# Three rational-function groups with b folded into two activation scales, and a new order of all steps

## The chip, the cores and the metric

One core of a Trainium2 chip runs the whole program. Its engines work side by side, each through its own list of instructions in order: TensorE (PE, matmuls into PSUM), VectorE (DVE), ScalarE (ACT), GpSimd (POOL, here mostly to start DMAs) and SyncE (SP, loads and stores). Semaphores tie them together. The metric is the device time of one execution in microseconds (us). Before the change the median of three runs is 264.83 us (264.46 to 264.94).

## The reference

```python
# attention with a polynomial feature map; q, k, v: (4 batches, 4 heads, 1088, 32), S1, S2: (8, 32)
def phi(x):
    a = einsum('rd,bhsd->bhsr', S1, x); b = einsum('rd,bhsd->bhsr', S2, x)
    return einsum('bhsi,bhsj->bhsij', a, b).reshape(..., 64)
kv  = einsum('bhsf,bhsd->bhfd', phi(k), v);  z = sum(phi(k), axis=2)
x   = einsum('bhsf,bhfd->bhsd', phi(q), kv) / (einsum('bhsf,bhf->bhs', phi(q), z) + 1e-6)
# then, over 4352 tokens of 128 features, w_in: (128, 2048), w_out: (2048, 128), a: (4,), b: (2,)
h = x @ w_in
P = a[0] + a[1]*h + a[2]*h**2 + a[3]*h**3
Q = 1 + |b[0]|*|h| + |b[1]|*h**2
out = (P / (Q + 1e-6)) @ w_out
```

## The kernel before, in words

The 4352 tokens are cut into ten chunks: two of 256 tokens, seven of 512, and one of 256 with the 64 leftover tokens of each batch. For each batch the key side (steps `k tr`, `k ev`, `k ab`, `k eva`, `k prod`, `kv`, `kv rem`, `kvbd`, `zbd`, `zproj`, `zspread`, `zrem`) builds kv and z; for each chunk the query side (`q tr`, `q ev`, `q abc`, `q eva`, for batches after the first a division `q dpr`, `q dsum`, `q dinv`, `q scale`, then `q prod`, `qp tr`, `qp ev`, `x mm`, `x ev`) gives the transposed x. The first two chunks, called 0 and 0b, go a slightly different way (`nd`, `div add`, `div inv`, `div`, `x tr`).

The second half works on groups: one chunk and up to eight blocks of 128 of the 2048 hidden features, so that a full group is a tile of 128 x 4096. There are 23 groups (0 to 22); 4 to 18 are full. A group g runs

- `h g,s` (PE, line 794): h = x @ w_in, two blocks at a time, into one of two PSUM tiles `h_ps`;
- `hev g,s` (ACT, line 800): h_ps to bf16 `hb`;
- the even part of Q into `u`, `ln g` and `exp g` (ACT, lines 833 and 837): u = exp(-ln(u + 1 + 1e-6)) = 1/Q;
- P into `y` (DVE), `n5 g` (DVE, line 829): y = y * u, and `py g` (PE, line 857): y @ w_out, summed in `out_ps`; then `oev`, `otr`, `otev` and a store.

The table `TERMS` gives each group one of four forms. Two matter here. Form "t" (groups 5, 7, 11, 13, 16, 18) takes |h| on DVE. Form "s" (groups 4, 9, 14) takes it on ACT. Before the change a group of form "s" has these steps:

- `habs` (ACT, line 809): u = |h * |b0||;
- `sq` (DVE, line 914): lin A = h * h;
- `sqb` (DVE, line 919): lin B = A * |b1|;
- `dq` (a DMA that POOL starts, line 897): u += B, after `habs` and `sqb`;
- `n1` (DVE, line 925): y = a3 * A + a1, and `n3` (DVE, line 925): A = a2 * A + a0, in place;
- `n2` (DVE): y = y * hb; `dy` (a DMA from POOL): y += A; then `ln`, `exp`, `n5`, `py`.

In form "t" the logarithm has a scale of its own, `b_rel[:, 0:1]`, a value per partition; in form "s" its scale is the constant 1. `lin` has two buffers, `hb`, `u` and `y` three each, `L` (between `ln` and `exp`) one.

Nothing is scheduled at run time. `plan.add` collects the steps in a fixed numbering, and `plan.issue` runs through the list `ORDER` and emits step after step, so `ORDER` alone decides in which order each engine meets its work. `HOT` is a list of blocks of dummy matmuls on a spare PSUM bank (`hot`, line 1075), which keep TensorE busy. b arrives by a load behind that of a (line 245); `abs_b` (line 387) and `rel_b` (lines 391 to 393) make |b0|, |b1| and the quotients from it.

Of the kernel before, what the change touches and what calls it, by code (L numbers as in the profile page):

```python
# [12 lines left out]
FP = mybir.dt.float32  # L13
BF = mybir.dt.bfloat16
# [5 lines left out]
    0, 2, 53, 4, 5, 1, 3, 54, 6, 8, 10, 55, 7, 9, 11, 12, 14, 13, 16, 15, 17, 70, 75, 56, 71, 18, 76, 72, 77, 52,  # L20
    19, 20, 73, 80, 22, 57, 24, 21, 23, 26, 25, 68, 78, 28, 69, 30, 74, 81, 97, 82, 27, 79, 85, 29, 98, 83, 84, 31,
    99, 86, 87, 88, 100, 101, 91, 102, 104, 89, 90, 103, 105, 106, 92, 113, 107, 108, 114, 109, 115, 110, 116, 111,
    117, 129, 112, 297, 60, 32, 130, 298, 118, 67, 119, 120, 65, 64, 311, 122, 121, 62, 34, 312, 123, 63, 299, 36,
    144, 325, 93, 124, 33, 125, 126, 319, 313, 61, 145, 66, 58, 127, 296, 300, 320, 146, 128, 301, 326, 94, 147,
    305, 302, 359, 321, 314, 95, 35, 306, 37, 96, 361, 38, 322, 315, 303, 316, 333, 40, 360, 200, 327, 334, 131,
    362, 317, 59, 148, 328, 363, 132, 307, 308, 365, 150, 304, 201, 39, 364, 133, 134, 309, 310, 162, 366, 318, 42,
    151, 135, 339, 136, 163, 323, 335, 137, 41, 43, 367, 329, 138, 324, 368, 369, 152, 153, 149, 166, 374, 336, 341,
    340, 167, 139, 342, 202, 154, 376, 140, 343, 155, 349, 141, 44, 142, 350, 375, 203, 351, 156, 330, 188, 157,
    158, 331, 143, 45, 189, 385, 337, 370, 377, 371, 190, 386, 159, 332, 352, 191, 387, 160, 204, 46, 161, 192, 164,
    344, 168, 378, 389, 372, 165, 388, 169, 391, 345, 211, 170, 171, 172, 390, 392, 407, 173, 174, 394, 338, 175,  # L30
    212, 48, 373, 393, 193, 177, 176, 408, 409, 346, 395, 178, 400, 379, 194, 411, 181, 410, 412, 179, 413, 195,
    182, 180, 432, 402, 50, 347, 401, 47, 414, 196, 348, 433, 353, 415, 354, 197, 215, 396, 49, 183, 403, 434, 198,
    397, 184, 398, 435, 404, 421, 416, 436, 438, 216, 437, 51, 439, 422, 417, 199, 423, 205, 441, 206, 399, 454,
    456, 440, 355, 185, 455, 442, 207, 237, 380, 238, 457, 405, 208, 424, 243, 209, 447, 458, 418, 210, 356, 460,
    448, 244, 381, 449, 213, 357, 425, 459, 214, 461, 217, 186, 218, 406, 443, 219, 462, 468, 450, 187, 479, 419,
    444, 480, 245, 445, 220, 481, 469, 382, 482, 483, 221, 463, 420, 246, 484, 426, 451, 222, 239, 247, 446, 501,
    485, 240, 486, 502, 464, 470, 427, 223, 452, 224, 505, 488, 489, 487, 490, 503, 225, 471, 504, 226, 494, 227,
    491, 230, 228, 507, 495, 428, 506, 229, 241, 526, 496, 465, 508, 358, 527, 453, 472, 528, 515, 530, 509, 466,
    467, 529, 383, 516, 510, 497, 473, 531, 532, 498, 548, 492, 231, 474, 533, 242, 232, 429, 517, 493, 233, 550,
    234, 549, 475, 511, 535, 551, 534, 536, 518, 512, 537, 541, 499, 235, 552, 553, 554, 236, 500, 543, 542, 248,  # L40
    538, 555, 519, 573, 513, 562, 575, 574, 476, 430, 556, 281, 576, 384, 577, 539, 544, 578, 563, 557, 545, 579,
    520, 558, 514, 564, 580, 282, 521, 565, 477, 582, 255, 249, 581, 583, 595, 540, 256, 250, 259, 251, 252, 596,
    588, 584, 253, 597, 254, 559, 257, 260, 601, 258, 589, 261, 590, 585, 546, 283, 598, 262, 263, 264, 522, 265,
# [80 lines left out]
def kernel(  # L124
# [13 lines left out]
    nc = tc.nc  # L138
# [23 lines left out]
    HOT = [2, 6, 23, 4, 18, 4, 3]  # L162
# [152 lines left out]
    b_rel = consts.tile([128, 3], FP, name="b_rel")  # L315
# [74 lines left out]
    def rel_b():  # L390
        nc.vector.tensor_scalar(out=b_rel[:, 0:1], in0=b_abs[:, 0:1], scalar1=1e-18, scalar2=None, op0=AX.max)
        nc.vector.reciprocal(out=b_rel[:, 1:2], in_=b_rel[:, 0:1])
        nc.vector.tensor_mul(out=b_rel[:, 2:3], in0=b_rel[:, 1:2], in1=b_abs[:, 1:2])

    c_b = plan.add("DVE", 100, abs_b, after=[ld["ab"]], rank=-5)
    c_b = plan.add("DVE", 300, rel_b, after=[c_b], rank=-5) if "t" in USED else c_b
# [187 lines left out]
    def add_queries(n, nt, srcs, weights, kv_lhs, load_steps, kv_steps, w_steps, rank, give=(), early=False,  # L584
# [58 lines left out]
        def product():  # L643
            abc = T["abc", n][:, :G, :]
            T["q_p", n] = tile_of(att, "q_p", [128, JC * H, R * R], FP)
            nc.vector.tensor_mul(out=T["q_p", n][:, :G, :].rearrange("p g (i j) -> p g i j", i=R),
                                 in0=abc[:, :, 0:R, None].broadcast_to([128, G, R, R]),
                                 in1=abc[:, :, None, R:2 * R].broadcast_to([128, G, R, R]))
# [69 lines left out]
        def rest(s):  # L718
            s = plan.add("DVE", 68 + 1067 * G // 16, product, after=[s, T.get(("prod", n - 1)) if pair == 1 else None], rank=rank + 0.02, take=["q_p"],
# [59 lines left out]
    def add_group(g, G):  # L779
# [27 lines left out]
        def s_abs():  # L807
            T["u", g] = tile_of(moe, "u", [128, GW], BF)
            nc.scalar.activation(out=T["u", g][:, :gw], in_=T["hb", g][:, :gw], func=ACT.Abs, scale=b_abs[:, 0:1])  # L809
# [21 lines left out]
        def ln(l0, lw):  # L831
            T["L", g, l0] = tile_of(moe, "L", [128, LW], FP)
            nc.scalar.activation(out=T["L", g, l0][:, :lw], in_=T["u", g][:, l0:l0 + lw], func=ACT.Ln, bias=one_ap,  # L833
                                 scale=b_rel[:, 0:1] if terms == "t" else 1.0)
# [278 lines left out]
```

## Time and profile before

| what | value |
|---|---|
| median of three runs | 264.83 us (264.46 to 264.94) |
| the profiled execution's own time | 264.85 us |
| its span, first to last instruction | 263.1 us, so 1.75 us lie around it |
| granted TensorE clock, mean | 0.996 |
| busy: PE, DVE, ACT, POOL | 246.8, 242.8, 238.6, 43.0 us |
| line 919, form "s" (`sqb`) | 3 instructions, 3.9 us |
| the software DMA queue | 25.69 MB, 62.6% of 16 DMA engines' span |

How to read it. A busy share is the time in which an engine executed something, so waiting is not in it; three engines are above 90% at once. "Idle before" tells how long an engine stood still ahead of an instruction and who released it. A mean duration overlaps a little with the next instruction on the same engine, so the distance from start to start is what an instruction really costs its engine. The windows view adds up busy time for stretches of the span; since it can count no more than the stretch, what is missing from a stretch is idle time.

### The profile page before, as it was taken

The numbers are of one execution on the slowest core, as the hardware profiler recorded it, in microseconds if no ns is written. First come the engines' busy times: TensorE is split into PE (matmuls) and PEld (weight loads), VectorE is DVE, ScalarE is ACT, GpSimd is POOL, SyncE is SP. The second block draws the span as 40 slices with busy tenths as digits, with TensorE's granted clock in tenths as the row PEclk, the third lists the DMA queues.
The fourth block names the chain that finished last, engine by engine and source line by source line (L and its number), as shares of the span: only waits on it lengthen the run. The fifth ranks groups of instructions, "written<-read, shape, count | busy, mean of one in ns | idle before, by whom it ended". The sixth has DMA issues, their size and how long they took to land. (4 is left out here: it accounts for less than half of the span.)

```text
span 263.1 us, 3159 instructions
## 1 busy us (share of the span) xinstructions
PE 246.8 (94%) x1186; PEld 145.6 (55%) x1186; DVE 242.8 (92%) x240; ACT 238.6 (91%) x211; POOL 43.0 (16%) x63
## 2 busy tenths in 40 slices
PE   8999999999999999989899998999999899999971
PEld 4889898755656654434373645545434345554451
DVE  1658999979999999999999999999999999999992
ACT  3249798889989999999999999999999999999993
POOL 3700010101201113011201121101220202122000
PEclk9999999999999999999999999999999999999998
DMA  6969839952888996938798879972799896788812
GB/s 171 298 209 174 166 90 173 218 91 50 189 159 96 165 190 93 118 55 150 144 133 139 156 102 181 184 139 50 133 167 128 159 187 84 91 159 162 120 40 101
DMA packets 36607, 36.94 MB, mean 140 GB/s; under 512 B 18160, under 2 KB 30448, under 8 KB 36464
## 3 DMA queue, kind: packets, MB, share of 16 engines
q0 software_dynamic: 11664, 25.69, 62.6%
q1 hardware_dynamic: 24496, 10.95, 15.8%
q8 instruction: 9, 0.15, 0.2%
q10 hardware_dynamic: 432, 0.10, 0.2%
q14 instruction: 6, 0.05, 0.1%
HBM read 8.82 MB, written 2.23 MB: 42 GB/s over the span
## 5 line engine op out<-in xcount | busy, mean ns | idle before, releaser
L794 PE MATMUL h_ps<-xT,w_in_sb 128*128 128x512 f32 (+1 forms) x320 | 126.6, 533 | 0.9 <-ACT hb L800 0.9
L794 PEld LDWEIGHTS h_ps<-xT,w_in_sb 128*128 128x128 f32 x320 | 57.4, 190 | 43.4 <-issue 34.3
L800 ACT CAST hb<-h_ps 128x1024 bf16<-128x1024 f32 (+1 forms) x70 | 70.9, 1038 | 5.6 <-PE h_ps L794 5.4
L837 ACT ACTIVATE u<-L 128x4096 bf16<-128x4096 f32 (+3 forms) x23 | 63.7, 2768 | 0.3
L829 DVE TENSOR_TENSOR y<-y,hb 128x4096 bf16<-128x4096 bf16 (+3 forms) x37 | 58.7, 1595 | 0.1
L833 ACT ACTIVATE L<-u,one_ap 128x4096 f32<-128x4096 bf16 (+3 forms) x17 | 43.4, 2555 | 0.2 <-DVE u L829 0.2
L829 DVE TENSOR_TENSOR y<-y,u 128x4096 bf16<-128x4096 bf16 (+3 forms) x23 | 39.8, 1731 | 0.5 <-ACT u L837 0.3
L857 PEld LDWEIGHTS <-w_out 128*128 128x128 bf16 x208 | 20.2, 98 | 27.6 <-issue 11.8
L857 PE MATMUL out_ps<-y,w_out 128*128 128x512 bf16 (+1 forms) x144 | 30.8, 355 | 1.1 <-DVE y L829 1.1
L897 POOL DMA_DIRECT2D u<-lin x9 | 10.8, 1206 | 104.4 <-ACT ab L461 25.7
L833 ACT ACTIVATE L<-u,one_ap,b_rel 128x4096 f32<-128x4096 bf16 x6 | 23.2, 3875 | 0.0
L914 DVE TENSOR_TENSOR lin<-hb 128x4096 bf16<-128x4096 bf16 x9 | 20.6, 2287 | 0.0
L897 POOL DMA_DIRECT2D y<-lin x9 | 12.0, 1334 | 49.6 <-DVE y L829 15.7
L829 DVE TENSOR_TENSOR u<-lin,u 128x4096 bf16<-128x4096 bf16 (+3 forms) x14 | 19.2, 1375 | 0.2
L897 POOL DMA_DIRECT2D y<-zeros x7 | 12.3, 1760 | 41.6 <-PE h_ps L794 18.4
L820 DVE TENSOR_SCALAR u<-hb 128x4096 int16<-128x4096 int16 (+3 forms) x20 | 18.4, 918 | 0.5 <-ACT hb L800 0.3
L489 PEld LDWEIGHTS kv_ps<-v_aug,k_p 128*128 128x128 f32 x128 | 15.3, 192 | 1.1 <-issue 0.2
L489 PE MATMUL kv_ps<-v_aug,k_p 128*128 128x66 f32 x128 | 15.8, 272 | 0.0
L857 PE MATMUL out_ps<-u,w_out 128*128 128x512 bf16 (+1 forms) x64 | 13.7, 352 | 1.3 <-ACT u L837 1.1
L1075 PE MATMUL kv_ps<-const-float32-0.0 128*128 128x512 bf16 x60 | 14.2, 381 | 0.0
L661 ACT COPY q_pT<-w_ps 128x512 f32<-128x512 f32 (+1 forms) x20 | 10.5, 552 | 2.6 <-PE w_ps L654 2.6
L841 DVE TENSOR_SCALAR y<-hb,a_sb 128x4096 bf16<-128x4096 bf16 (+3 forms) x14 | 12.4, 886 | 0.0
(102 smaller groups left out, 274.1 us busy)
## 6 DMA issues: line engine op xcount, KB each, us to landing
u<-lin POOLq DMA_DIRECT2D x9, 1024.0 KB, 7.9
y<-lin POOLq DMA_DIRECT2D x9, 1024.0 KB, 8.2
y<-zeros POOLq DMA_DIRECT2D x6, 1024.0 KB, 11.0
out_dram<-oT SPq DMA_DIRECT2D x7, 256.0 KB, 2.7
kq<-in_k_dram SPq DMA_DIRECT2D x3, 512.0 KB, 5.0
v_aug<-in_v_dram SPq DMA_DIRECT2D x12, 128.0 KB, 4.7
kq<-in_q_dram SPq DMA_DIRECT2D x3, 512.0 KB, 4.8
w_in_sb<-in_moe_w_in_dram SPq DMA_DIRECT2D x1, 1024.0 KB, 6.9
```

Source lines behind the costliest of these rows:

```text
L489: nc.tensor.matmul(T["kv", b][:, hp * 66:(hp + 1) * 66], lhsT=lhs(hp), rhs=rhs(hp), start=(first and hp == 0), stop=final, skip_group_chec ...
L794: nc.tensor.matmul(T["h", g, s][:, i * W:(i + 1) * W], lhsT=w_in_sb[:, fi * 128:(fi + 1) * 128], rhs=T["xT", n][:, :W], start=True, stop=True)
L800: nc.scalar.copy(out=T["hb", g][:, s * W:(s + nsub) * W], in_=T["h", g, s][:, :nsub * W])
L820: nc.vector.tensor_scalar(out=u().bitcast(mybir.dt.int16), in0=hb().bitcast(mybir.dt.int16), scalar1=0x7FFF, scalar2=None, op0=AX.bitwise_and)
L829: return lambda: nc.vector.tensor_mul(out=out(), in0=in0(), in1=in1())
L833: nc.scalar.activation(out=T["L", g, l0][:, :lw], in_=T["u", g][:, l0:l0 + lw], func=ACT.Ln, bias=one_ap, scale=b_rel[:, 0:1] if terms == ...
L837: nc.scalar.activation(out=T["u", g][:, l0:l0 + lw], in_=T["L", g, l0][:, :lw], func=ACT.Exp, scale=-1.0)
L841: nc.vector.tensor_scalar(out=y(), in0=hb(), scalar1=a_sb[:, 3:4], scalar2=a_sb[:, 2:3], op0=AX.mult, op1=AX.add)
L857: nc.tensor.matmul(T["o", n][:, :W], lhsT=W_terms[w][:, fis[i], :], rhs=T[src, g][:, i * W:(i + 1) * W], start=(start and i == 0), stop=(s ...
L897: nc.gpsimd.dma_start(out=dst(), in_=src(), accum_op=AX.add, max_dma_last_dim=4096)
L914: nc.vector.tensor_mul(out=sq(), in0=hb(), in1=hb())
L1075: nc.tensor.matmul(hot_ps[0], lhsT=zero.broadcast_to([128, 128]), rhs=zero.broadcast_to([128, CW]), start=True, stop=True)
```

## The change

In a group of form "s" Q is divided by |b1| inside: `habs` takes |h| times |b0|/|b1| (`b_rel[:, 5:6]`), the DMA `dq` adds the square itself, and `ln` multiplies by |b1| (`b_rel[:, 1:2]`, a value per partition). `sqb` is gone from the three groups. The square must now outlive `n3`, so `n3` writes its result into the second `lin` buffer, `dq` waits for `n3`, and `dy` adds that second buffer. `rel_b` makes six values with four instructions in place of three values with three. A choice `QPOOL` is added and left empty. `HOT` has 11 blocks with 71 dummy matmuls in place of 7 with 60. `ORDER` is a new list; here are the moves that matter, by engine:

- DVE: `abs_b` and `rel_b` go ahead of `q prod 0b` (before: `abs_b` right behind it, `rel_b` much later); the first steps of groups 0 and 1 are mixed anew; `k prod (3, 0)` goes ahead of `sq 9`; `n5` of groups 4, 7, 16, 18 and some `abs`, `n1` change places with neighbours.
- ACT: `ln 0`, `exp 0` ahead of `hev 2,0`; `k ev ('rem', 1)`, `q ev 2` later; `qp ev 3,1`, `q ev 4`, `oev 0` ahead of `hev 7,4`; `exp 12` ahead of `q eva 8`; `hev 10,0` behind `habs 9`; `hev 19,4` ahead of `ln 17`, so that `exp 17` follows `ln 17` directly.
- PE: `h 3,2` ahead of `h 3,0`; `kv 3,0`, `kv 3,1`, `kv rem 3` of the last batch much earlier, among the blocks of groups 10 and 11 (before: groups 12 to 14), so that `h 10,4` to `h 12,0` stand further back; `hot 0` already among the blocks of group 14 (before: group 17).
- POOL: the copy for `zproj` behind two copies of v. SP: two stores change places; the loads are as before.

```diff
 ORDER = [
...
-    HOT = [2, 6, 23, 4, 18, 4, 3]
+    QPOOL = set()
+    HOT = [5, 4, 1, 6, 3, 19, 13, 6, 7, 4, 3]
...
-    b_rel = consts.tile([128, 3], FP, name="b_rel")
+    b_rel = consts.tile([128, 6], FP, name="b_rel")
...
     def rel_b():
-        nc.vector.tensor_scalar(out=b_rel[:, 0:1], in0=b_abs[:, 0:1], scalar1=1e-18, scalar2=None, op0=AX.max)
-        nc.vector.reciprocal(out=b_rel[:, 1:2], in_=b_rel[:, 0:1])
-        nc.vector.tensor_mul(out=b_rel[:, 2:3], in0=b_rel[:, 1:2], in1=b_abs[:, 1:2])
+        nc.vector.tensor_scalar(out=b_rel[:, 0:2], in0=b_abs[:, 0:2], scalar1=1e-18, scalar2=None, op0=AX.max)
+        nc.vector.reciprocal(out=b_rel[:, 2:4], in_=b_rel[:, 0:2])
+        nc.vector.tensor_mul(out=b_rel[:, 4:5], in0=b_rel[:, 2:3], in1=b_abs[:, 1:2])
+        nc.vector.tensor_mul(out=b_rel[:, 5:6], in0=b_rel[:, 3:4], in1=b_abs[:, 0:1])
...
         def s_abs():
             T["u", g] = tile_of(moe, "u", [128, GW], BF)
-            nc.scalar.activation(out=T["u", g][:, :gw], in_=T["hb", g][:, :gw], func=ACT.Abs, scale=b_abs[:, 0:1])
+            nc.scalar.activation(out=T["u", g][:, :gw], in_=T["hb", g][:, :gw], func=ACT.Abs, scale=b_rel[:, 5:6])
...
             nc.scalar.activation(out=T["L", g, l0][:, :lw], in_=T["u", g][:, l0:l0 + lw], func=ACT.Ln, bias=one_ap,
-                                 scale=b_rel[:, 0:1] if terms == "t" else 1.0)
+                                 scale={"t": b_rel[:, 0:1], "s": b_rel[:, 1:2]}.get(terms, 1.0))
...
         if square:
             sp = plan.add("DVE", tt, s_first, after=[he], rank=g - 0.5, take=["lin"], name=f"sq {g}")
-            d2 = plan.add("DVE", ts + 61, s_scaled, after=[sp, c_b], rank=g - 0.5, take=["lin"], name=f"sqb {g}")
-            d = add_tile("dq", u, even, [ha, d2], g - 0.5, give=["lin"])
+            if wide_abs:
+                d1 = plan.add("DVE", ts + 121, s_affine(y, 3, 1), after=[sp, ld["ab"]], rank=g - 0.45, take=["y"], name=f"n1 {g}")
+                t = plan.add("DVE", ts + 121, s_affine(even, 2, 0), after=[sp, d1, ld["ab"]], rank=g - 0.45, take=["lin"], name=f"n3 {g}")
+                d = add_tile("dq", u, sq, [ha, t], g - 0.5, give=["lin"])
+            else:
+                d2 = plan.add("DVE", ts + 61, s_scaled, after=[sp, c_b], rank=g - 0.5, take=["lin"], name=f"sqb {g}")
+                d = add_tile("dq", u, even, [ha, d2], g - 0.5, give=["lin"])
...
-            p = add_tile("dy", y, sq, [p, t], g - 0.3, give=["lin"])
+            p = add_tile("dy", y, even if wide_abs else sq, [p, t], g - 0.3, give=["lin"])
```

## The prediction

> **What bounds the kernel now.** I read the busy totals first.
>
> ```profile
> PE 246.8 (94%) x1186; PEld 145.6 (55%) x1186; DVE 242.8 (92%) x240; ACT 238.6 (91%) x211; POOL 43.0 (16%) x63
> ```
>
> Three engines are above 90%, so no total decides; the windows view (stretch; its length; busy time of PE, PEld, DVE, ACT, POOL; clock; DMA share; GB/s) shows who fills which stretch.
>
> ```profile
> 30.00:40.00 10.00, 10.00 (x72) 9.24 (x71) 9.75 (x15) 8.43 (x10) 1.31 (x1) 1.00 0.59 113
> 40.00:50.00 10.00, 10.00 (x62) 7.40 (x61) 9.96 (x15) 7.83 (x12) 1.20 (x1) 1.00 1.06 202
> 50.00:60.00 10.00, 10.00 (x53) 6.47 (x52) 8.64 (x10) 9.16 (x8) 0.00 (x0) 1.00 0.68 115
> 70.00:80.00 10.00, 10.00 (x58) 6.83 (x56) 10.00 (x7) 9.29 (x10) 3.26 (x2) 1.00 0.72 147
> 110.00:120.00 10.00, 8.75 (x29) 3.91 (x28) 9.96 (x8) 10.00 (x9) 1.17 (x1) 1.00 0.48 80
> 150.00:160.00 10.00, 9.61 (x41) 4.88 (x40) 10.00 (x6) 10.00 (x9) 1.81 (x1) 1.00 0.87 119
> ```
>
> PE is full from 20 to 100 us. ACT still has holes up to about 57 us and hardly one afterwards: over the windows from 60 to 250 us its idle time adds up to 1.86 us (0.71 in 70 to 80, 0.19 and 0.06 in the next two, nothing from 100 to 170, 0.22, 0.18, 0.18 from 170 to 200, 0.23 in 210 to 220, 0.09 elsewhere). DVE is as full, with 1.2 us idle there. So there are two regimes: PE sets the pace up to the last eviction of group 5, then ACT and DVE together. The ACT timeline names what its holes wait for.
>
> ```profile
> 47.71 1.01 ACT L800 CAST hb<-h_ps 128x1024 bf16<-128x1024 f32 x1 [1.18 <-PE h_ps L794]
> ...
> 56.12 1.01 ACT L800 CAST hb<-h_ps 128x1024 bf16<-128x1024 f32 x1 [0.70 <-PE h_ps L794]
> ...
> 78.89 1.01 ACT L800 CAST hb<-h_ps 128x1024 bf16<-128x1024 f32 x1 [0.70 <-PE h_ps L794]
> ```
>
> Each one waits for a matmul of line 794 that PE reached too late, none for DVE.
>
> **The change part by part.** The sum is made against the profiled execution's own 264.85 us (span 263.1 plus 1.75 around it), 0.02 us above the median, 264.83.
>
> *The removed multiplication.* The instructions by shape:
>
> ```profile
> L919 DVE TENSOR_SCALAR lin<-lin,b_abs 128x4096 bf16<-128x4096 bf16 x3 | 3.9, 1285 | 0.1
> L833 ACT ACTIVATE L<-u,one_ap 128x4096 f32<-128x4096 bf16 x9 | 34.1, 3793 | 0.0
> L833 ACT ACTIVATE L<-u,one_ap,b_rel 128x4096 f32<-128x4096 bf16 x6 | 23.2, 3875 | 0.0
> ```
>
> Line 919 costs 1.20 us from its start to the next start (178.97 to 180.17), so DVE loses 3 x 1.2 = 3.6 us of work. None of it is ACT's or PE's. The first 1.2 (group 4, at 36 us) lies in PE's stretch: DVE already waits 1.19 us at 54.30 for an eviction of ACT that follows PE, and it would only wait longer. The other 2.4 lie where ACT has no time free. I therefore book the cut itself at 0; its ends are -3.6 (all of it on the path) and 0.
>
> *The front.* Up to the matmuls `h 5,6` PE has the same work in another order, and the rows of PE from 18 to 57 us stand without a hole, so order alone cannot bring `hev 5,6` forward. One wait can push it back. Reading DVE's timeline and the loads:
>
> ```profile
> 16.32 0.42 DVE L696 TENSOR_TENSOR o_sb<-w_ps,den 128x256 f32<-128x256 f32 x1
> 16.89 0.69 DVE L646 TENSOR_TENSOR q_p<-abc 128x512 f32<-128x512 f32 x1 [0.15 <-ACT abc L618]
> 17.68 0.17 DVE L387 TENSOR_SCALAR b_abs<-b_sb 128x2 int32<-128x2 int32 x1
> ...
> 14.45 0.43 SPq L245 DMA_DIRECT2D b_sb<-in_moe_b_dram  x1
> ...
> b_sb<-in_moe_b_dram SPq DMA_DIRECT2D x1, 1.0 KB, 3.2
> ```
>
> b lands at 14.45 + 3.2 = 17.65, and `abs_b` starts at 17.68: it waits for the load. Now `abs_b` and the four of `rel_b` stand ahead of `q prod 0b`. DVE stands still from 16.74 to 17.68, then spends 0.19 on each of four dependent small ones (start to start at 22.58, 22.77, 22.96) and 0.08 on the last (0.08 behind 22.96): `q prod 0b` starts at about 18.5 rather than 16.89 and ends at 19.15. Queued behind it on DVE are `zbd 0`, `w1`, the first steps of group 0; for it waits `qp tr 0b,0` on PE, which started at 18.93, with PE full behind it. PE loses about 0.25. Ends: 0 (b lands a little earlier) and +1. Behind that DVE has its old holes (0.30 at 19.75, 1.13 at 21.27) to catch up.
>
> *ACT from 57 us on.* Its work is the same but for two things. Three logarithms get a pointer scale: from start to next start 3.71 us with it (182.10 to 185.81) against 3.61 without (197.35 to 200.97), so +0.3; ends +0.25 (three times 3875 - 3793 ns) and +0.3. And `exp 17` now follows its own logarithm: `ln 16` did so and took 3.88 (220.96 to 224.84) against 3.71, so +0.15.
>
> The gain must come from its holes. The new order puts `qp ev 3,1` (0.48), `q ev 4` (0.48) and `oev 0` (0.25) ahead of the two waits at 77.17 and 78.89, work that stood behind them: of 0.86 about 0.7 is filled. `exp 12` ahead of `q eva 8`, `hev 10,0` behind `habs 9` (which waited for a buffer) and PE's earlier blocks of the last batch (no `kv rem 3` in front of `h 14,0` any more) act on the small ones. DVE, 1.2 to 3.6 us ahead, delivers sooner to the matmuls `py` in front of the next `h`. Ends: 0 and -1.86; I take -1.4, nearer to the lower end, since the largest hole is filled with a known row.
>
> *The DMAs.* Same sizes. `dq` waits for `n3` (1.25 + 1.25 behind `sq`) where it waited for `sqb` (1.2), but in groups 9 and 14 the logarithm starts at 128.76 and 197.35, long after the landings some 8 us behind 114.91 and 180.79. In group 4 it is close: POOL's `dq` at 38.61 becomes about 39.2, the landing 48.5, and `ln 4` started at 48.88. 0, with up to +0.5 if it slips, most of it covered by the wait at 56.12. What `lin` frees is the same: one buffer behind `dq`, one behind `dy`. On POOL and SP only what waits for loads and stores anyway changes place: 0.
>
> *The dummies.* 11 more at 0.216 are 2.4 us of PE, all behind 160 us, where PE's windows to 250 leave 4.9 us idle: 0; without that cover 2.4.
>
> *PE between 100 and 138 us.* The last batch's `kv` work moves ahead of the blocks of groups 10 to 12; `h 12,0` stands 6.8 us of PE work further back, `h 12,2` 1.9. Before, PE lost 2.8 us in waits there (the steps from 101.96, 112.32, 114.70 and 124.32 took 2.05, 2.38, 1.40 and 2.61 where 1.73, 1.72, 0.44 and 1.72 are their work). If the moved work fills these, `h 12,0` comes 4.0 later against a slack of 5.6 (end 132.09, eviction 137.73), and `h 12,2` in time. I take +0.2; ends 0 and +2.0, worked out below.
>
> *The tail.* Behind `exp 18` (ended 246.03) DVE and ACT alternate. DVE's work from there on falls by 0.4 (one `n3` of group 20 goes ahead). I take -0.3; the rest of DVE's lead ends in a wait for `exp 18`.
>
> Sum: +0.25 + 0.3 + 0.15 - 1.4 + 0.2 - 0.3 = -0.8, to 264.05; since the front term and the last term are upper guesses of small waits, with 0.1 and 0.1 in their place it is -1.05. I forecast **263.9 us** (-0.95). Its own range is 263.2 (all holes filled) to 264.3.
>
> **The rivals.**
> *DVE was the bound.* It is as full as ACT, and the chain that ended last runs over it from 145 to 172 us. Then 3.6 come off: 261.2. Against: ACT has 1.86 us of holes in 190. 0.06.
> *Nothing is squeezed.* PE is late at the same places, and the terms +0.25 + 0.3 + 0.15 - 0.3 remain: 265.25. For: every hole waits for PE, which gets no less to do. 0.17.
> *PE becomes the bound between 100 and 138 us* (the other side). If PE still loses its 2.8 in waits there, `h 12,0` ends at 132.1 + 6.8 = 138.9, 1.6 past its eviction, and `h 12,2` at 138.68 + 1.92 = 140.6, where ACT comes at 139.11 - 0.47: 2.0 us of wait on an engine with nothing free. -0.95 + 2.0 is about +1: 265.85. It decides from 0.8 us of remaining waits. For: matmuls `py` wait in order for DVE's `n5`, and `n5 7` now stands behind `k prod (3, 1)` and `q prod 5`. Against: the moved work is just what can run in those waits. 0.20.
> *PE cools in the tail.* In the rows the granted clock is 1.00 in every window and 0.92 only in the last, while PE never stands still for more than some 1.5 us. Between `h 21,0` and `py 18` 18 dummies become 7 and 4, and PE stands still for up to 18 - 11 = 7 of them, 1.5 us, plus the 0.8 it lost there before: 2.3 us. If that sufficed to halve the clock, `py 18` (1.72) and the last `py 22` (0.4) would double: +0.4 to +2.1, so 264.3 to 266. The Trainium skill (TensorE: Matmul & The Clock Gate, Part 1: The HAM clock gate) says that the array falls to half its clock after an idle window of about 3.4 us; by that rule 2.3 us cost nothing. No wait of that length stands in this trace, so the rule is not shown here. 0.07.
>
> **How the numbers follow.** Forecast 0.50, the rivals 0.06, 0.17, 0.20, 0.07. 0.2% is 0.53 us, about what this kernel's runs can tell from no change: faster is below 264.3, slower above 265.4. Faster: 0.50 + 0.06 + 0.02 of the cool tail = 0.58. Same: 0.13 of the unsqueezed case and 0.03 of the tail = 0.16. Slower: 0.20 + 0.04 + 0.02 = 0.26. The range from 262.6 to 265.7 leaves out DVE's full cut (0.06) and about half of PE's case (0.10).
>
> **What would show it.** Line 919 with six instructions; line 833 with nine of the `b_rel` form at 3.87; DVE idle some 3 us more, in waits for ACT and PE; the wait at 78.89 below 0.2; `abs_b` at 17.7 with about 1 us idle before it and `q prod 0b` at 18.5. The forecast is wrong if ACT's holes between 60 and 250 us stay at 1.9 or grow, above all before the evictions of groups 11 and 12, or if DVE stays full and the span falls by 3.

## The result and the profile after

The changed kernel takes 265.37 us (median; 265.14 to 266.88), the kernel before on the same chip 264.69. The ratio is 1.0033, 95% interval 1.0021 to 1.0045: slower by a third of a per cent, where 0.95 us less was forecast. The time lies inside the range, on the wrong side of no change. The profiled execution took 265.57 us, its span is 263.9.

The busy totals of the changed kernel, and its windows (stretch; its length; busy time of PE, PEld, DVE, ACT, POOL; clock; DMA share; GB/s):

```profile
PE 249.6 (95%) x1185; PEld 146.8 (56%) x1197; DVE 240.0 (91%) x238; ACT 238.7 (90%) x211; POOL 40.8 (15%) x63
```

```profile
30.00:40.00 10.00, 10.00 (x64) 9.06 (x63) 9.72 (x12) 8.57 (x9) 0.91 (x1) 1.00 0.43 83
40.00:50.00 10.00, 10.00 (x70) 7.65 (x70) 8.00 (x12) 7.63 (x13) 1.60 (x2) 1.00 0.96 185
...
70.00:80.00 10.00, 9.70 (x46) 5.61 (x45) 10.00 (x8) 9.49 (x12) 0.86 (x2) 1.00 0.77 153
...
110.00:120.00 10.00, 10.00 (x47) 5.61 (x46) 9.89 (x7) 10.00 (x7) 2.37 (x2) 1.00 0.61 104
...
150.00:160.00 10.00, 9.90 (x39) 5.02 (x40) 10.00 (x6) 10.00 (x10) 1.81 (x1) 1.00 0.94 150
...
180.00:190.00 10.00, 9.95 (x32) 4.69 (x32) 7.72 (x8) 9.41 (x10) 2.38 (x2) 1.00 0.76 138
```

DVE is 2.8 us less busy, and its idle time has two new places: 2.0 us between 40 and 50 us, 2.3 between 180 and 190. ACT's busy total is what it was. Between 60 and 250 us ACT stands still for 1.78 us, where it was 1.86: the holes add up to nearly as much as before, in other places. Its timeline:

```profile
56.62 1.01 ACT L803 CAST hb<-h_ps 128x1024 bf16<-128x1024 f32 x1 [0.70 <-PE h_ps L797]
...
73.19 3.80 ACT L836 ACTIVATE L<-u,one_ap,b_rel 128x4096 f32<-128x4096 bf16 x1 [0.51 <-DMA u<-lin]
...
79.97 1.01 ACT L803 CAST hb<-h_ps 128x1024 bf16<-128x1024 f32 x1
...
176.47 0.59 ACT L718 COPY xT<-w_ps 128x512 f32<-128x512 f32 x1 [0.25 <-PE w_ps L670]
...
182.24 1.01 ACT L803 CAST hb<-h_ps 128x1024 bf16<-128x1024 f32 x1 [0.19 <-PE h_ps L797]
...
189.93 1.01 ACT L803 CAST hb<-h_ps 128x1024 bf16<-128x1024 f32 x1 [0.40 <-PE h_ps L797]
...
257.22 0.72 ACT L836 ACTIVATE L<-u,one_ap 128x512 f32<-128x512 bf16 x1 [0.47 <-DVE u L832]
```

The 0.70 us that stood ahead of `hev 7,6` (now at 79.97) are gone, as forecast. In their place stand 0.51 ahead of `ln 5` at 73.19, for a landing, then waits for PE at 176, 182 and 190, and a longer wait in the tail. The groups by shape, as in the prediction:

```profile
L836 ACT ACTIVATE L<-u,one_ap,b_rel 128x4096 f32<-128x4096 bf16 x9 | 34.6, 3842 | 0.5 <-DMA u<-lin 0.5
L836 ACT ACTIVATE L<-u,one_ap 128x4096 f32<-128x4096 bf16 x6 | 22.5, 3745 | 0.0
...
L921 DVE TENSOR_SCALAR lin<-lin,b_rel 128x4096 bf16<-128x4096 bf16 x6 | 7.7, 1284 | 0.1
```

Nine logarithms with a pointer scale, 97 ns longer each, and six `sqb` left of nine. DVE's timeline shows the wait for b in front, and ahead of `n1 15` a wait of 2.28 us for `hev 15,6` of ACT, where the kernel before has none:

```profile
17.71 0.17 DVE L388 TENSOR_SCALAR b_abs<-b_sb 128x2 int32<-128x2 int32 x1 [0.91 <-DMA b_sb<-in_moe_b_dram]
...
18.47 0.69 DVE L649 TENSOR_TENSOR q_p<-abc 128x512 f32<-128x512 f32 x1
...
188.80 1.34 DVE L844 TENSOR_SCALAR y<-hb,a_sb 128x4096 bf16<-128x4096 bf16 x1 [2.28 <-ACT hb L803]
```

The same `n1 15` in the kernel before, and in two kernels of the next section, `e1_cut_only` and `e11_new_middle`:

```profile
187.81 1.35 DVE L841 TENSOR_SCALAR y<-hb,a_sb 128x4096 bf16<-128x4096 bf16 x1
187.74 1.35 DVE L844 TENSOR_SCALAR y<-hb,a_sb 128x4096 bf16<-128x4096 bf16 x1 [1.26 <-ACT hb L803]
187.03 1.34 DVE L844 TENSOR_SCALAR y<-hb,a_sb 128x4096 bf16<-128x4096 bf16 x1 [1.23 <-ACT hb L803]
```

From `n1 15` on DVE sets the pace. Up to its last instruction of group 22 it stands still for about 1 us in 70, and the span ends 75.05 us behind `n1 15` in the changed kernel, 75.33 in the kernel before, 75.09 and 75.08 in the other two. So the time is settled at `n1 15`, by whichever comes later there: DVE's own work, or ACT with `hev 15,6`. In the kernel before the two meet. All three cuts lie ahead of this point, so DVE alone gains nothing by them; `hev 15,6` has to come earlier too, and in the changed kernel it comes later.

### The profile page after: what moved, and what is told of

It is laid out like the page before. It is cut to its first block, busy times and chain, and to the rows that moved or that the text cites. A ratio compares the mean times of both kernels' runs of the same rounds, so it can differ in the third digit from the quotient of the medians.

```text
span 263.9 us, 3176 instructions
## 1 busy us (share of the span) xinstructions
PE 249.6 (95%) x1185; PEld 146.8 (56%) x1197; DVE 240.0 (91%) x238; ACT 238.7 (90%) x211; POOL 40.8 (15%) x63
## 4 chain that ended last, share of the span: by engine, by line
PE 43%; ACT 21%; DVE 14%; DMA 8%; issue 8%; SPq 5%; ACTq 0%
PE h_ps L797 22%; ACT L L836 9%; DMA u<-lin 7%; PE out_ps L860 6%; DVE y L832 6%; ACT hb L803 5%; ACT u L840 4%; PE kv_ps L491 4%; PE w_ps L609 2%; PE w_ps L657 2%; SPq L246 2%; PE w_ps L455 2%; PE w_ps L670 2%; DMA b_sb<-in_moe_b_dram 1%; DVE lin L828 1%
## 5 line engine op out<-in xcount | busy, mean ns | idle before, releaser
L836 ACT ACTIVATE L<-u,one_ap,b_rel 128x4096 f32<-128x4096 bf16 x9 | 34.6, 3842 | 0.5 <-DMA u<-lin 0.5
L836 ACT ACTIVATE L<-u,one_ap 128x4096 f32<-128x4096 bf16 (+3 forms) x14 | 31.7, 2268 | 0.5 <-DVE u L832 0.5
L860 PE MATMUL out_ps<-y,w_out 128*128 128x512 bf16 (+1 forms) x137 | 30.2, 354 | 1.8 <-DVE y L832 1.2
L900 POOL DMA_DIRECT2D y<-zeros x7 | 11.4, 1633 | 49.3 <-DVE y L832 31.8
L1084 PE MATMUL kv_ps<-const-float32-0.0 128*128 128x512 bf16 x69 | 17.0, 381 | 0.1
L900 POOL DMA_DIRECT2D y<-lin x9 | 10.7, 1191 | 36.6 <-PE h_ps L797 11.2
```

Source lines behind the costliest of these rows:

```text
L860: nc.tensor.matmul(T["o", n][:, :W], lhsT=W_terms[w][:, fis[i], :], rhs=T[src, g][:, i * W:(i + 1) * W], start=(start and i == 0), stop=(s ...
L900: nc.gpsimd.dma_start(out=dst(), in_=src(), accum_op=AX.add, max_dma_last_dim=4096)
L1084: nc.tensor.matmul(hot_ps[0], lhsT=zero.broadcast_to([128, 128]), rhs=zero.broadcast_to([128, CW]), start=True, stop=True)
```

## The experiments

`ORDER` is a list of numbers; in the diffs the steps stand by name. "Against before" is the median less that of the kernel before on the same chip, which differs a little from one set of runs to the next (264.69 to 264.89). On that scale the changed kernel is at +0.68, and differences between two kernels below some 0.2 us tell little. Single profiled executions differ too: in the seven that share the changed kernel's front, `hev 0,0` starts between 18.85 and 19.59 us. Timelines are therefore compared from a step that both have in common.

**The edit without the new order.** Everything but `ORDER` and `HOT` is as in the changed kernel.

```diff
 on DVE, in the order of before, g = 4, 9, 14:
   sq g,
-  sqb g, ... n1 g, ... n3 g
+  n1 g, n3 g
```

> The changed code (no `sqb` in groups 4, 9, 14, `b_rel` with six columns, pointer scale in three logarithms) in the order of the kernel before: `n1` and `n3` of those groups stand where `sqb` stood, the seven blocks of dummies and `abs_b`/`rel_b` are where they were. Theory (ACT and PE set the pace, DVE's 3.6 us are not on the path, the loss of the change lies in the new order): the time of before, 264.7, plus up to 0.3 for three pointer scales, less whatever a lighter DVE squeezes: 264.4 to 265.0. Rival 1 (the edit itself harms, since `dq` starts 1.3 us later behind `n3`): 265.3 or more, like the changed kernel. Rival 2 (DVE was the bound and the new order gives its gain away): 261.2 to 262.5.

264.76 us, 0.09 under before, ratio 1.0003 (0.9995 to 1.0012). The edit is worth nothing in the old order. ACT's holes from 57 to 250 us are 1.66 here. By the trace it is not the cut alone that is near nothing, but a small sum: the pointer scales make ACT 0.10 later at `ln 4`, `ln 9` and `ln 14` each, the first of which is gone at `hev 5,4`, and from `n1 15` to the end the kernel takes 75.09 us where it took 75.33. DVE's freed time becomes waits: 1.26 us ahead of `n1 15`, 1.80 at `q dpr 3` where it was 1.19. The whole loss belongs to the new order.

**DVE's work put back into the new order.**

```diff
 def f():   # of n3, form "s"
+    nc.vector.tensor_scalar(out=out(), in0=sq(), scalar1=b_rel[:, 4:5], scalar2=None, op0=AX.mult)
     nc.vector.tensor_scalar(out=out(), in0=sq(), scalar1=a_sb[:, c1:c1 + 1], scalar2=a_sb[:, c0:c0 + 1], ...
```

> The changed kernel with one multiplication of 128x4096 on DVE put back in each of groups 4, 9 and 14, just ahead of `n3` (its result is overwritten): DVE has the 3.6 us again, `dq` 1.2 us later. Theory (DVE's work is not on the path in the new order either): 265.4 to 266.0. Rival (the new order has DVE on the path, and without the cut it would have been far slower): 267.5 to 269.

268.82 us, ratio 1.0151 (1.0136 to 1.0166), 3.29 us over the changed kernel on the scale above. My theory fell. The same work that was free to go in the old order cannot be put back into the new one. But 3.29 is no price of 3.6 us of work: by the trace ACT goes from 0.34 ahead to 2.19 late between 45 and 48 us (group 4, with a stretch at half clock, see **Group 4 alone**), falls back by 0.96 at 125 to 127 (group 9) and by 0.28 at 190 (group 14), for 1.2 us of work each.

**The wait for b.**

```diff
 on DVE:
   div 0,0,
-  abs_b, rel_b, q prod 0b
+  q prod 0b, abs_b, rel_b
```

> The changed kernel with `abs_b` and `rel_b` moved behind `q prod 0b` on DVE, nothing else. Theory (PE is the only engine without a hole up to 57 us and the wait for b delays it): the 0.25 to 0.5 us that PE is late at `hev 5,6` come off the end: 264.9 to 265.1. Rival (the delay is caught up in later holes of ACT, or `zbd 0` and `k` work is now late by the same time): 265.3 to 265.5.

265.17 us, ratio 1.0013 (1.0002 to 1.0024): +0.32 against before, so 0.36 less than the changed kernel. In the trace `q prod 0b` starts at 16.95 in place of 18.47, and ACT is 0.34 us ahead from 24 us on and 0.41 ahead at 190; nothing catches up such a delay in front. The time lies between the two ranges. How large the delay is hangs on when b lands. From `hev 0,0` to `hev 5,6` every profile with the old front takes 36.98 to 37.00 us. With the new front it is 37.11 in `e10_pe_more`, where b is there in time (`abs_b` does not wait); 37.43 in the changed kernel (it waits 0.91); 37.83 in `e4_const_scale` (1.30); and 37.11 here. So the order costs 0.12 by itself, and the wait for b, in the profiles, up to 0.7 more.

**The pointer scale.**

```diff
-    scale={"t": b_rel[:, 0:1], "s": b_rel[:, 1:2]}.get(terms, 1.0)
+    scale={"t": b_rel[:, 0:1], "s": 1.0}.get(terms, 1.0)
```

> The changed kernel with a constant scale of 1.0 in the logarithms of groups 4, 9 and 14 in place of the pointer (this leaves the factor |b1| out of the three groups' denominators). Theory (ACT has no time free behind 57 us): two or three times 0.1 us come off: 265.05 to 265.2. Rival (ACT's holes take it up): 265.3 to 265.5.

This kernel leaves the factor |b1| out of the three groups' denominators, so it only prices the operand. 265.15 us, ratio 1.0017 (1.0007 to 1.0027): +0.30 against before, 0.38 less than the changed kernel. The trace does not bear out that the operand costs this much. ACT gains 0.09 at `ln 4` and `ln 9` and has lost it again at `hev 5,6` and `hev 12,0`; 0.16 come from a shorter wait for a landing at `ln 5` (0.35 for 0.51); the 0.10 of `ln 14` lie behind `n1 15`, from where both kernels take 75.05 us. The profiled execution is 0.13 shorter.

**One hole filled, in the old order.** This is the failed step by itself.

```diff
 on ACT, in the order of e1_cut_only:
   q ev 5, hev 7,4,
+  oev 0, qp ev 3,1,
   hev 7,6, exp 5,
-  oev 0, qp ev 3,1,
   hev 8,0, k ev (3,0), hev 8,2
```

> The kernel `e1_cut_only` (changed code, order of before) with two evictions, `oev 0` and `qp ev 3,1`, moved on ACT from behind `exp 5` to ahead of `hev 7,6`, where ACT waits 0.70 us for PE; nothing else. It asks the step of the prediction that failed, whether a hole of ACT that is filled with known work shortens the end. Theory of the prediction (ACT has no other time free behind it): 0.5 to 0.6 off, 264.15 to 264.3. Rival (PE is late everywhere there, and what is filled here opens again at the next evictions, `k ev (3,0)` and `hev 8,2` first): 264.6 to 264.9, with the holes of ACT from 57 to 250 us still at about 1.6.

264.78 us, ratio 0.9997 (0.9988 to 1.0006): nothing. ACT's timeline of `e1_cut_only`, and then that of this kernel:

```profile
78.70 1.01 ACT L803 CAST hb<-h_ps 128x1024 bf16<-128x1024 f32 x1 [0.70 <-PE h_ps L797]
...
85.09 0.59 ACT L450 COPY kT<-w_ps 128x512 f32<-128x512 f32 x1 [0.19 <-PE w_ps L445]
```

```profile
78.38 0.60 ACT L664 COPY q_pT<-w_ps 128x512 f32<-128x512 f32 x1
78.92 1.01 ACT L803 CAST hb<-h_ps 128x1024 bf16<-128x1024 f32 x1
...
85.31 0.58 ACT L450 COPY kT<-w_ps 128x512 f32<-128x512 f32 x1 [0.96 <-PE w_ps L445]
```

The hole is filled, and ACT is 0.76 us ahead at the end of `hev 8,0` (timelines set level at `hev 6,6`). Six microseconds later it waits 0.96 where it waited 0.19: the whole gain is given back, and from there to 130 us the two timelines run level to 0.01. At 85 us PE is still the engine that sets the pace, and a hole of ACT there is only the sign of it.

**More work for PE.** The changed kernel with one matmul of 0.86 us done twice, once at 78 us and once at 140.

```diff
-    for i in range(nsub):
+    for i in [0] + list(range(nsub)) if (g, s) == (7, 6) else range(nsub):    # e16: (13, 0)
```

> The changed kernel with the first of the two matmuls of `h 7,6` done twice (0.86 us more on PE at about 78 us, the second overwrites the first). Theory (PE sets the pace up to some 95 us in the new order too): 0.6 to 0.9 slower than the changed kernel, 266.0 to 266.3. Rival (ACT is the bound from 57 us on, as the prediction had it, and PE has time): 265.3 to 265.6.

> The changed kernel with the first matmul of `h 13,0` done twice: the same 0.86 us on PE as in `e10_pe_more`, but at about 140 us. Theory (PE sets the pace only up to some 95 us; later it waits for ACT and DVE): 265.3 to 265.6, no slower than the changed kernel. Rival (PE is on the path there too, as in the rival of the prediction for 100 to 138 us): 266.0 to 266.3.

At 78 us: 266.30, ratio 1.0070 (1.0049 to 1.0090), 0.93 over the changed kernel, all of the 0.86. At 140 us: 266.17, ratio 1.0060 (1.0042 to 1.0079), 0.60 over it. The second is against my theory: I had PE free there. ACT's lines of the two:

```profile
80.58 1.01 ACT L803 CAST hb<-h_ps 128x1024 bf16<-128x1024 f32 x1 [0.77 <-PE h_ps L797]
```

```profile
150.42 1.01 ACT L803 CAST hb<-h_ps 128x1024 bf16<-128x1024 f32 x1 [0.43 <-PE h_ps L797]
```

From start to start ACT falls back by 0.86 us at the first place, which is all of the work, and by 0.59 at the second (a wait of 0.77 or 0.43 costs some 0.1 more than its length, the overlap with the eviction ahead of it). So PE has nothing to spare at 80 us and 0.3 at 150.

**ACT relieved, DVE loaded.** Group 14 in form "t".

```diff
-    **{g:"s" for g in (4,9,14)}, **{g:"t" for g in (5,7,11,13,16,18)}
+    **{g:"s" for g in (4,9)}, **{g:"t" for g in (5,7,11,13,14,16,18)}
 on DVE, in the order of e1_cut_only:
-  sq 14, q dinv 8, q scale 8, n1 14, n3 14, n5 12, n2 14
+  sq 14, abs 14, sqb 14, q dinv 8, q scale 8, n5 12, n1 14, n3 14, n2 14
```

> The kernel `e1_cut_only` with group 14 in the form of groups 5 to 18 that take the absolute value on DVE: ACT loses `habs 14` (3.76), DVE gains `abs 14` and `sqb 14` (1.22 + 1.28). Of the 3.6 us that the cut freed on DVE this uses 2.5. If ACT alone set the pace and DVE's free time could be used: 261.0 to 262.5. If DVE is as much on the path (each waits for the other, and the free time lies in places where it cannot be used): between no change and the 2.5 of DVE, 264.5 to 267.3. My own theory lies between, some 1 us off: 263.5 to 264.3, with new waits of ACT for DVE behind 185 us.

265.68 us, ratio 1.0033 (1.0020 to 1.0047): 0.84 slower than before, though ACT has 3.76 us less to do. My own theory missed. ACT's timeline:

```profile
179.19 1.01 ACT L803 CAST hb<-h_ps 128x1024 bf16<-128x1024 f32 x1 [2.39 <-PE h_ps L797]
180.91 1.01 ACT L803 CAST hb<-h_ps 128x1024 bf16<-128x1024 f32 x1 [0.70 <-PE h_ps L797]
...
214.64 1.01 ACT L803 CAST hb<-h_ps 128x1024 bf16<-128x1024 f32 x1 [1.29 <-PE h_ps L797]
```

The time taken from ACT comes back as waits for PE, 2.39 and 0.70 at once, and 1.29 at `hev 18,2`, since DVE is 1.16 us late from `n1 15` on. `hev 15,6` comes 0.25 us earlier than in `e1_cut_only` and `n1 15` waits for nothing; it now starts at 188.91 because DVE has more to do ahead of it, and the end lies 75.08 us behind it, as there (75.09). ACT is not the bound behind 188 us; DVE is.

**The new order in pieces.** The two orders were spliced at evictions that both have done at that point.

```diff
 e7:  order of the changed kernel to hev 5,6   | that of e1_cut_only to the end
 e8:  that of e1_cut_only to hev 5,6           | that of the changed kernel to the end
 e11: e1_cut_only to hev 5,6 | changed to hev 11,6 | e1_cut_only to the end
 e12: e1_cut_only to hev 5,6 | changed to exp 15   | e1_cut_only to the end
```

> The order of the changed kernel up to `hev 5,6`, and from there the order of `e1_cut_only` with its seven blocks of dummies. Theory (the new front alone costs what PE is late at `hev 5,6`, and behind it nothing is caught up): 264.76 + 0.35 to 0.5 = 265.1 to 265.3. Rival (the front's delay is caught up in ACT's holes at 78.9 and later): 264.7 to 264.9.

> The order of `e1_cut_only` up to `hev 5,6` (without `q tr 4`, which keeps its place in the new order), and from there the order and the eleven blocks of the changed kernel. Theory (what the new order fills at 78.9 it loses again at `ln 5`, `hev 15,2`, `hev 16,0` and in the tail): 264.7 to 265.1. Rival (the squeeze of the prediction is there, and only the new front hid it): 264.0 to 264.4.

> The order of `e1_cut_only` up to `hev 5,6`, that of the changed kernel to `hev 11,6`, and from there that of `e1_cut_only` again with its seven blocks. In `e8_new_rest` ACT was 0.3 us ahead of `e1_cut_only` at `hev 11,6`. Theory (a lead of ACT at 130 us survives, and the new order loses it behind 138 us): 264.4 to 264.6. Rival (DVE, which sets the pace from 145 us on, takes it back whatever the order): 264.7 to 265.0.

> The kernel `e8_new_rest` up to `exp 15`, and from there the order of `e1_cut_only` (the logarithm of group 17 apart from its exponential, the old order of groups 19 to 22) with seven blocks of dummies in all. Theory (the new tail costs about 0.25: 0.16 where `exp 17` follows its own logarithm, the rest in front of `ln 22`): 264.7 to 264.8. Rival (the tail is the same length in both): 264.95 to 265.1.

| kernel | median | against before | ratio, 95% interval |
|---|---|---|---|
| e1_cut_only | 264.76 | -0.09 | 1.0003 (0.9995 to 1.0012) |
| e11_new_middle | 264.10 | -0.59 | 0.9979 (0.9970 to 0.9987) |
| e12_old_tail | 264.71 | +0.02 | 1.0003 (0.9994 to 1.0012) |
| e8_new_rest | 265.01 | +0.17 | 1.0006 (0.9997 to 1.0015) |
| the changed kernel | 265.37 | +0.68 | 1.0033 (1.0021 to 1.0045) |
| e7_new_front | 266.62 | +1.78 | 1.0071 (1.0055 to 1.0086) |

Read downwards, each row of the first five adds one stretch of the new order: the middle (57 to 132 us) brings 0.50, the stretch from 132 to 215 costs 0.61, the tail 0.15, the front 0.51. `e11_new_middle` is the fastest kernel of the case, faster than its theory had it. For the first two stretches the traces, set level at `hev 5,6`, say a gain of 0.64 and a loss of 0.64. The tail's 0.15 is below what the runs can tell. The front's 0.51 is not all the front's: `e8_new_rest` and the changed kernel have one order from `hev 5,6` on, the profiles put 0.45 between them up to there, and 0.29 more at one landing, which stays to the end:

```profile
72.68 3.80 ACT L836 ACTIVATE L<-u,one_ap,b_rel 128x4096 f32<-128x4096 bf16 x1 [0.22 <-DMA u<-lin]
```

This is `ln 5` in `e8_new_rest`; in the changed kernel it waits 0.51. (The execution of `e8_new_rest` had started 0.23 later, so that 0.52 is left between the spans.) `e7_new_front` says nothing on the front: at the splice `q ev 4` waits 1.58 us for `q tr 4`, which the new order had put off, so the splice made that loss, and its median lies outside both ranges.

Where the stretch from 132 to 215 us loses is seen between `e11_new_middle` and `e12_old_tail`, set level at `hev 5,6`. At `hev 14,6`, with the same steps done, the second is 0.23 ahead; at `hev 15,6`, four evictions later, it is 0.97 late. Between them it waits 0.25 for `x mm 6` and 0.19 for `h 15,2`, as the changed kernel does in the lines shown, where the old order waits for nothing; and the new order puts `qp ev 7,0`, some 0.5 us, ahead of `hev 15,2`, where the old one has it behind `hev 15,6`. The wait of 0.40 ahead of `hev 16,0` comes behind `hev 15,6` and holds up `n1 15` no more. On PE `qp tr 7,0` stands ahead of `pr 12`, `h 15,0` and `h 15,2` in the changed kernel and starts when DVE's `q prod 7` is done, at 176.33. What each of these moves costs alone was not tried.

**The new middle without the cut.** The code of before, with `sqb`, in the order of `e11_new_middle`.

```diff
 on DVE, in the order of e11_new_middle:
   sq 9,
+  sqb 9,
   n1 9, n3 9       (groups 4 and 14 as the kernel before has them)
```

> The code of the kernel before (with `sqb` in groups 4, 9 and 14 and no pointer scale there) in the order of `e11_new_middle`: `sqb` 4 and 14 with their `n1` and `n3` where the kernel before had them, `sqb 9` between `sq 9` and `n1 9`. Theory (the new middle is faster only because DVE has the cut to spend: the 2.4 us of groups 9 and 14 are then on the path): 265.3 to 266.5. Rival (the order of PE and ACT between 57 and 132 us brings the 0.66 us, and the cut has nothing to do with it): 264.0 to 264.4.

265.32 us, ratio 1.0016 (1.0008 to 1.0025): 0.43 slower than before. So the edit alone gives 0.09, this order alone costs 0.43, and both together give 0.59: in this order the cut, with its pointer scales, is worth 1.02 us (1.18 by the traces). In this kernel DVE is late itself: `n1 15` starts at 188.30 with a wait of 0.04, where it waited 1.23 for ACT in `e11_new_middle`.

**What the new middle does.** By three other orders of PE between 78 and 98 us in `e5_fill_hole`, one corrected after the other; in `e9_pe_ahead` evictions of ACT and steps of DVE move with them.

```diff
 on PE:
   h 7,4, h 7,6,
-  kv 2,1, kv rem 2, h 8,0, h 8,2, k tr (3,0), py 4, ..., q abc 4, q abc 5, x mm 3, py 5, h 9,0
+  h 8,0, h 8,2, kv 2,1, kv rem 2, k tr (3,0), py 4, ..., x mm 3, q abc 4, h 9,0, q abc 5, py 5     (e9)
+  (as e9) ..., x mm 3, q abc 4, py 5, h 9,0, q abc 5                                               (e14)
+  (as e9) ..., x mm 3, py 5, h 9,0, q abc 4, q abc 5; on ACT hev 9,0 ahead of q eva 4, 5           (e17)
```

> The kernel `e5_fill_hole` with PE's work between 78 and 96 us in another order: `h 8,0` and `h 8,2` ahead of `kv 2,1` and `kv rem 2`; `x mm 3` ahead of `q abc 4`; `q abc 5` and `py 5` behind `h 9,0`. The evictions follow: `k ev (3,0)` behind `hev 8,2`, `x ev 3` and `exp 6` ahead of `q eva 4` and `q eva 5`; on DVE `kvbd 2` behind `sqb 7`, `q dpr 5` and `q dsum 5` behind `n2 8`. No work is added or left out. Theory (up to about 95 us PE sets the pace, a hole of ACT filled there only opens again behind the next matmul, and what counts is which matmul PE does first): the 0.96 us in front of `k ev (3,0)` goes and about 0.6 is left at `ln 7`: 264.1 to 264.3. Rival (DVE or a landing takes it back behind 100 us, as full as they are): 264.6 to 264.9.

> The kernel `e9_pe_ahead` with `py 5` back ahead of `h 9,0`. In `e9_pe_ahead` ACT had come 1.0 us ahead at `hev 9,0` as expected, but `n1 8` on DVE waited 1.90 us for the buffer of `y` that `py 5` frees, and from there on DVE was 1.3 us late to the end. Theory (PE's order sets the pace up to 95 us, and the loss was this wait alone): the lead stays, 264.1 to 264.4. Rival (DVE is late without that wait too): 264.7 to 265.3.

> The kernel `e14_py5_back` with both `q abc 4` and `q abc 5` on PE behind `h 9,0`, and on ACT `hev 9,0` ahead of `q eva 4` and `q eva 5`, as the changed kernel has them. In `e14_py5_back` ACT's lead of some 1 us at 92 us ended in a wait of 0.89 for `q abc 5`; PE had the same matmuls to do ahead of `hev 9,0` as before. Theory (what counts up to 98 us is how much work of PE stands ahead of the next `h`; 1.9 us less of it leaves ACT 0.4 to 0.9 ahead at `ln 7`, and with DVE's cut that lead lasts to the end): 263.9 to 264.3. Rival (the gain of `e11_new_middle` came from its order of DVE behind 100 us): 264.6 to 264.8.

Measured: `e9_pe_ahead` 265.88 (ratio 1.0045, 1.0032 to 1.0058), `e14_py5_back` 264.67 (0.9992, 0.9983 to 1.0000), `e17_q_behind` 264.41 (0.9989, 0.9979 to 0.9999). The line of DVE that spoilt the first, and the lines of ACT where the second and the third lose their lead:

```profile
97.65 1.34 DVE L844 TENSOR_SCALAR y<-hb,a_sb 128x4096 bf16<-128x4096 bf16 x1 [1.90 <-PE out_ps L860]
```

```profile
97.91 0.48 ACT L620 COPY abc<-w_ps 128x384 f32<-128x384 f32 x1 [0.89 <-PE w_ps L609]
```

```profile
108.30 1.93 ACT L803 CAST hb<-h_ps 128x1024 bf16<-128x1024 f32 x2 [1.00 <-PE h_ps L797]
```

All three bring ACT some 0.9 to 1.0 us ahead behind 92 us, as the theory had it. In the first `n1 8` waits 1.90 for a buffer of `y` that `py 5` frees, and DVE stays 1.2 us late to the end, with the time: once DVE is late behind 100 us, nothing makes it good. In the second the lead ends at `q abc 5`, because PE had to do the same matmuls ahead of the next eviction as before. In the third it ends at `h 9,6`. From there on all of it is gone: set level at `hev 7,6`, the second kernel ends 0.05 behind `e5_fill_hole` and the third level with it. The third's median is 0.43 under before, but of the 0.38 by which its profiled execution is shorter than that of `e5_fill_hole` 0.37 stand already at `hev 0,0`, ahead of everything that its edit touches. All three medians miss the ranges of the theory. So these orders do not show what the new middle gains by; its order of DVE behind 100 us is left as the rival, and it was not tried alone.

**Group 4 alone.** As `e2_extra_mult`, in one group.

```diff
+    if out is even and g == 4:
+        nc.vector.tensor_scalar(out=out(), in0=sq(), scalar1=b_rel[:, 4:5], scalar2=None, op0=AX.mult)
```

> The changed kernel with the extra multiplication of 128x4096 on DVE in group 4 alone (of the three in `e2_extra_mult`). There `k prod` came later, PE stood still for 0.60 us at 43.0, and in the profiled run the granted clock was 0.50 from 46.1 to 49.5 us; ACT was 2.2 us late behind it. Theory (group 4 alone makes about two thirds of the 3.4 us): 267.0 to 267.6, the granted clock again at 0.50 for 3.4 us in most runs. Rival (the wait and the slow stretch came from all three): 265.4 to 266.0 at a clock of 1.00.

267.85 us, ratio 1.0113 (1.0098 to 1.0127), 2.28 over the changed kernel for 1.2 us of work, more than the theory's range. PE's timeline (start, duration) and the windows of one microsecond:

```profile
43.76 2.00 PE L491 MATMUL kv_ps<-v_aug,k_p 128*128 128x66 f32 x16 [0.60 <-DVE k_p L474]
```

```profile
43.00:44.00 1.00, 0.40 (x3) 0.24 (x3) 1.00 (x2) 1.00 (x2) 0.87 (x1) 1.00 0.97 168
44.00:46.00 2.00, 2.00 (x19) 1.93 (x18) 1.03 (x2) 1.12 (x3) 0.33 (x1) 1.00 1.19 197
46.00:47.00 1.00, 1.00 (x7) 0.88 (x6) 0.57 (x3) 0.00 (x0) 0.00 (x0) 0.58 0.95 78
47.00:48.00 1.00, 1.00 (x6) 0.99 (x5) 0.96 (x2) 0.04 (x1) 0.00 (x0) 0.50 0.73 124
48.00:49.00 1.00, 1.00 (x2) 0.34 (x1) 0.74 (x1) 1.00 (x3) 0.00 (x0) 0.50 1.09 383
```

DVE's `k prod` comes later, PE stands still for 0.60 us, and from 46.2 to 49.6 us the clock (the third number from the end) is at 0.50. The cut in group 4, which I had booked as a longer wait of DVE and nothing else, keeps the changed kernel away from this in its own order.

## Why the prediction was wrong

- *The removed multiplication, 0.* Right for what it said: the edit in the old order gives -0.09. It left out that a new order can spend the freed time. `e2_extra_mult` finds 3.29 us for putting the work back into the new order, 2.28 of them in group 4 with its stretch at half clock (`e15_extra_g4`); `e13_middle_no_cut` prices the edit at 1.02 in the new middle alone. The rival "DVE was the bound" holds from `n1 15` on, but the cut lies ahead of it, where DVE then waits for ACT.
- *ACT from 57 us on, "I take -1.4".* This is the step that failed. The known row did fill the hole at 78.9, and ACT's holes still add up to 1.78. The error lies in the two regimes. PE sets the pace further than to 57 us: the one hole that was filled by itself opened again behind it at 85 us (`e5_fill_hole`: 0.76 won, 0.77 given back), and in `e17_q_behind` a lead of 0.99 ended at 108. Where this ends is not shown. The windows view had said it, PE full from 20 to 100 us; I took the lack of holes in ACT behind 57 us as the mark of the bound. And the second regime is not ACT and DVE together: behind `hev 15,6` DVE alone decides, so only an earlier `hev 15,6` counts, with DVE ready for it, and holes behind it count for nothing. The new middle does bring it forward, by 0.61 us in `e11_new_middle` against `e1_cut_only`, and the moves at 175 to 182 us put it 1.20 back.
- *The front, +0.25 with ends 0 and +1.* Each step came as written: `abs_b` at 17.71, 0.91 us of waiting, `q prod 0b` at 18.47. PE is 0.50 late at `hev 5,6`, twice the term, and `e3_b_later` gives 0.36 of it back. The step is partly luck: of the kernels with this front two, `e2_extra_mult` and `e10_pe_more`, had b in time in their profiles and did not wait. The "old holes to catch up" were DVE's, and PE, which had none, kept the delay.
- *The pointer scale, +0.3, and `exp 17` behind its logarithm, +0.15.* Both hold for ACT: 97 ns for each of the three logarithms, and `exp 17` starts 3.76 us behind its own (230.63 to 234.39), where one of that kind followed by other work took 3.61. As terms of the sum they fail: `ln 14` and `ln 17` stand behind `n1 15`, where DVE sets the pace, and `ln 4` ends in a wait for PE. The 0.38 of `e4_const_scale` is not found in its trace. The Trainium skill (ScalarE: Activation LUTs, What ACT_TABLE_LOAD costs) gives about 93 ns for a pointer operand; the rows agree with 97.
- *The DMAs, 0 with up to +0.5.* The slip came, not in group 4 but in 5: `dq 5` landed after 10.06 us where it had taken 8.59, and `ln 5` waited 0.51. It is on the path: between `e8_new_rest` and the changed kernel 0.29 more of this wait put the end 0.3 later. In every profile with this part of the new order the landing took 9.8 to 10.1 us and `ln 5` waited 0.22 to 0.51; with the old order it took 8.5 to 8.7 and nothing waited.
- *PE between 100 and 138 us, +0.2.* `hev 12,2` waits 0.03 us; the rival built on it did not come. But `e16_pe_more_late` shows that PE has only 0.3 us to spare at 150 us.
- *The tail, -0.3.* Wrong sign: ACT's idle time from 250 us on grows from 4.70 to 5.02, with `ln 22` waiting 0.47 for DVE where it waited 0.21. The splice puts 0.15 on the new tail; but from `n1 15` to the end the changed kernel takes 75.05 us, 0.28 less than before and as long as `e1_cut_only` (75.09; `e12_old_tail` 74.81), so the loss of the change is not made here. ACT's waits in the tail are for DVE.
- *The dummies, 0.* Not tried alone. `hot 1`, four dummies, ends ahead of `x mm 6`, which then waits for ACT's `qp ev 6,1`; `e12_old_tail`, which has no dummies there, has the same 0.25 ahead of `x ev 6`.
- *The cooling tail.* The clock is 1.00 to the last window and 0.92 in it, as before.
- *The sum.* It gives -0.8, and -1.05 with 0.1 for the front and 0.1 for the +0.2 of PE (not for the last term, the tail). The forecast of -0.95 lies between them without a reason, and the lower end of its own range is 263.34 by the terms, not 263.2.

The front's 0.51, the stretch from 132 to 215 us with 0.61 and the tail's 0.15 against 0.50 from the middle and 0.09 from the edit make +0.68, as measured (the rows are differences of one table, so they must). "Nothing is squeezed", 265.25, is nearest in time and in its word that every hole waits for PE; it had PE late at the same places, and they are others, so its 0.12 from the measured time is luck.

## What to carry to other kernels

Ask of a hole whose lateness it shows: where the engine that it waits for is itself full, filling the hole can only move it to the next wait. Where three engines are above 90%, look for the step from which one engine runs to the end almost without a wait, and ask what reaches that step last: freed time counts only if everything that reaches it comes earlier. And splice an old and a new order at a few common points, and keep the stretches that gain.

## What the runs showed that I had not expected

- A standstill of PE of 0.60 us was followed, some 2.5 us after its end, by 3.41 us at half clock, in both profiles in which it stood at 43 us. A longer one of the changed kernel brought nothing, the clock stays at 1.00:

```profile
163.05 1.13 PE L609 MATMUL w_ps<-W_abc,qT 128*128 128x96 f32 x8 [1.06 <-ACT qT L603]
```

  The Trainium skill (TensorE: Matmul & The Clock Gate, Part 1: The HAM clock gate) lets the clock fall after an idle window of about 3.4 us, counted in windows that run on by themselves. The length of the slow stretch agrees, 3.41 us; no idle window stands ahead of it by the rows, PE being busy for all but 0.60 us. What sets the two cases apart was not tried. Nor is it settled what share of the 2.28 us is the clock's: of the four runs of `e15_extra_g4` three have a mean clock of 0.991 and take 267.81 to 268.27, and one has 0.996 and takes 267.56; of the four of `e2_extra_mult` three have 0.988 or 0.989 and take 268.76 to 269.17, and one has 0.997 and takes 268.26. A stretch of 3.41 us at half clock lowers the mean by 0.006, so the two have none, and they are only 0.25 to 0.91 us faster: most of the loss is there without it.
- Work and order do not add up. The edit by itself gives 0.09, the new middle by itself loses 0.43, and together they gain 0.59. At `n1 15` the reason is seen: with the edit alone DVE waits there 1.26 for ACT, with the order alone DVE has no time to wait and starts it at 188.30, and only with both does it start sooner, at 187.03.
- A landing can slip by more than its issue: `dq 5` was issued 0.60 us later (63.03 after 62.43) and landed 2.07 later. The load of q behind it on another queue was issued 0.51 us after it in place of 1.04.
